# Linear term of the first batch by another route, and the weights' transposes moved into the main loop

## The chip, the cores and the metric

The kernel runs on one core of a Trainium2 chip. The metric is the device time of one execution in microseconds. Three runs of the kernel before took 329.71, 330.14 and 330.32 us; the median, 330.14 us, is what a prediction is measured against. A traced execution of its own spans 328.5 us, and the TensorE clock granted in it was full (1.00) from end to end.

Engines are named as the profile names them: PE is TensorE's matmul, PEld its weight load, DVE is VectorE, ACT is ScalarE, POOL is GpSimd, SP is SyncE.

## The reference

Four batches of N = 12544 rows of C = 128 columns go through an attention with m = 32 inducing rows, twice, and then through a two-branch maxout layer.

```python
scale = 1.0 / np.sqrt(C)
def mab(q, kv):
    s = scale * (q @ kv.transpose(0, 2, 1))
    s = s - s.max(-1, keepdims=True)
    a = np.exp(s)
    a /= a.sum(-1, keepdims=True) + 1e-09
    return a @ kv
h = mab(I, x)              # (B, 32, 128): the inducing rows attend to x
y = mab(x, h)              # (B, N, 128): x attends to h
h1, h2 = y @ w1, y @ w2    # w1, w2: 128 x 1024
out = np.maximum(h1, h2) @ w_out   # w_out: 1024 x 128
```

The kernel uses max(h1, h2) = h1 + relu(h2 - h1), and that y = a h with a of only 32 columns. With e the unnormalised second attention,

```
out = [ relu(e (h (w2 - w1))) w_out  +  e (h w1 w_out) ] / rowsum(e)
```

h (w2 - w1) is a 32 x 1024 matrix for each batch, called hwd. h w1 w_out is a 32 x 128 matrix for each batch, called m1: the linear term.

## The kernel before

Rows are taken in chunks of 128, and chunks in blocks of up to 16, split into four quarters of up to four chunks. Each quarter has its own 32 rows of the PE array.

The order of all instructions is worked out by the program as it is built, with a small clock model `ck` of PE, ACT, DVE and the eight PSUM banks. Its durations are constants in the code; they order the instructions and choose between ACT and DVE, and they synchronise nothing. The parts of a block:

- `stage(blk)`: scores of the block, four column-tiled matmuls, then exp on ACT into the tile `e2`;
- `phase(jobs)`: up to four jobs, one for each quarter, side by side on the array. A job "U" makes a PSUM bank of e2 · hwd, which ACT or DVE turns into relu (16 bit) in SBUF; a job "L" makes the linear term of a group;
- `final_one`: one matmul of a relu piece with w_out into the bank of its group (a quarter's chunks), eight for each chunk;
- `evict_group`: DVE multiplies by the reciprocal of the row sum, and SP stores.

A group's bank is first written by its "L" job, so its finals come after that. Only block 0's first group adds its linear term at the end. Where PE would wait for a bank, `keep_busy` fills with matmuls on a tile `warm`.

The weights of batch 0 (cuts are marked "..."):

```python
w2h = relup.tile([128, 4096], F16, name="w2h", tag="relu0")[:, 0:J]
w1h = relup.tile([128, 4096], F16, name="w1h", tag="relu1")[:, 0:J]   # pool relup: bufs=2 for each tag
...
def small_hwd(b, halves=(0, 1)):
    ...
    for half in halves:
        for n in range(2 if b == 0 and half == 0 else 1):
            w = 256 if b == 0 and half == 0 else 512
            ...
            if b == 0:
                nc.tensor.matmul(out=ps, lhsT=st[b]["hT4"], rhs=w2h[:, sl], start=True, stop=False)
                nc.tensor.matmul(out=ps, lhsT=st[b]["hT4"], rhs=w1h[:, sl], start=False, stop=True)
            ...
            if half == 0 and n == 0:
                ...   # DVE evicts
            else:
                ...   # ACT evicts
def small_m1(b):
    ...
    nc.tensor.matmul(out=ps[:, 0:128], lhsT=st[b]["hT4"], rhs=w1out, start=True, stop=True)
    ...               # DVE evicts to m1, and for batch 0 to m1bd as well
def weights_2():      # w1T: eight transposes of w1h, evicted half by DVE, half by ACT
    ...
def weights_3():      # w1out = w1 w_out: eight matmuls with w1T, evicted by ACT
    ...
```

w1h is negated in place on DVE before these run. The start of the main loop:

```python
nc.vector.tensor_scalar(out=w1h, in0=w1h, scalar1=-1.0, scalar2=None, op0=ALU.mult)
sums = small_h(0)
weights_2()
small_sums(*sums)
stage(blocks[0])
small_hwd(0, (0,))
blocks[0].staged = max(blocks[0].staged, st[0]["hwdr"])
small_hwd(0, (1,))
stage(blocks[1])
...
phase(plan_phase(False))
weights_3()
phase(plan_phase(False))
pending.append((small_m1, (0,)))
state["stage"] = 2
weights_1b()
while state["g"] < len(groups) or held:
    ...   # phases, finals, stages and the next batches' first attention, by ck
```

How a relu is given to an engine:

```python
if max(ck.act, ready) + 0.477 <= max(ck.dve, ready) + 0.597:
    nc.scalar.activation(out=dst, in_=src, func=AF.Relu)
    t = ck.on_act(ready, 0.477)
else:
    nc.vector.tensor_scalar(out=dst, in0=src, scalar1=0.0, scalar2=None, op0=ALU.max)
    t = ck.on_dve(ready, 0.597)
```

Of the kernel before, what the change touches and what calls it, by code (L numbers as in the profile page):

```python
# [9 lines left out]
F16 = mybir.dt.float16  # L10
F32 = mybir.dt.float32
AF = mybir.ActivationFunctionType
ALU = mybir.AluOpType
# [3 lines left out]
INF = 1e9  # L17
# [85 lines left out]
def kernel(  # L103
# [9 lines left out]
    nc = tc.nc  # L113
    B, N, C = x.shape
    M = inducing.shape[0]
# [26 lines left out]
    def bank(shape, dtype=F32, only=None):  # L142
        i = min(range(8), key=lambda j: ck.bank[j]) if only is None else only
        uid[0] += 1
        return i, psum.tile(shape, dtype, name=f"ps{uid[0]}", tag=f"bank{i}", bufs=1)
# [51 lines left out]
    with tc.manual_schedule(engines={ET.PE, ET.DVE, ET.Activation, ET.Pool, ET.SP}):  # L197
# [247 lines left out]
            nc.vector.tensor_scalar(out=st[0]["rw"], in0=st[0]["rs"], scalar1=1.0 / scale, scalar2=None, op0=ALU.mult)  # L445
            ck.bank[st[0]["eb"]] = st[0]["rsr"] = ck.on_dve(end, 0.34)

        def small_hwd(b, halves=(0, 1)):
            if 0 in halves:
                st[b]["hwd"] = smp.tile([128, J], F16, name=f"hwd_{b}", tag="hwd")  # L450
            hwd = st[b]["hwd"]
            for half in halves:
                for n in range(2 if b == 0 and half == 0 else 1):
                    w = 256 if b == 0 and half == 0 else 512
                    bi, ps = bank([128, 512])
                    ps = ps[:, 0:w]
                    sl = slice(512 * half + w * n, 512 * half + w * (n + 1))
                    ck.wait(max(ck.bank[bi], st[b]["hT4r"]), "p1")
                    if b == 0:
                        nc.tensor.matmul(out=ps, lhsT=st[b]["hT4"], rhs=w2h[:, sl], start=True, stop=False)  # L460
                        nc.tensor.matmul(out=ps, lhsT=st[b]["hT4"], rhs=w1h[:, sl], start=False, stop=True)
                        end = ck.run(0.43 * w / 512)
                    else:
                        nc.tensor.matmul(out=ps, lhsT=st[b]["hT4"], rhs=w21[:, sl], start=True, stop=True)  # L464
                        end = ck.run(0.215)
                    if half == 0 and n == 0:
                        if b == 0:
                            nc.vector.tensor_scalar(
                                out=hwd[:, sl], in0=ps, scalar1=st[0]["rw"], scalar2=None, op0=ALU.mult
                            )  # L470
                        else:
                            nc.vector.tensor_copy(out=hwd[:, sl], in_=ps)
                        ck.bank[bi] = ck.on_dve(end, 0.07 + w / 970.0)
                    else:
                        nc.scalar.activation(
                            out=hwd[:, sl], in_=ps, func=AF.Copy, scale=st[0]["rw"] if b == 0 else 1.0
                        )
                        ck.bank[bi] = ck.on_act(end, 0.06 + w / 1200.0)
                    st[b]["hwdr"] = max(ck.bank[bi], st[b].get("hwdr", 0.0))

        def small_m1(b):
            bi, ps = bank([128, 512])
            ck.wait(max(ck.bank[bi], st[b]["hT4r"]), "p1")
            nc.tensor.matmul(out=ps[:, 0:128], lhsT=st[b]["hT4"], rhs=w1out, start=True, stop=True)
            end = ck.run(0.06)
            m1 = smp.tile([128, C], F16, name=f"m1_{b}", tag="m1")
            bd = {0: [0], B - 1: [0, 1, 2, 3]}.get(b, [])
            outs = [(m1bd[32 * q : 32 * (q + 1), q, :], slice(32 * q, 32 * (q + 1))) for q in bd]
            for o, r in outs + [(m1, slice(0, 128))]:
                if b == 0:  # L490
                    nc.vector.tensor_scalar(
                        out=o, in0=ps[r, 0:128], scalar1=st[0]["rw"][r, :], scalar2=None, op0=ALU.mult
                    )
                else:
                    nc.vector.tensor_copy(out=o, in_=ps[r, 0:128])
                ck.bank[bi] = ck.on_dve(end, 0.2)
            st[b]["m1"] = m1
            st[b]["m1r"] = ck.bank[bi]
# [13 lines left out]
            for h in range(2):  # L512
                nc.gpsimd.tensor_sub(w21[:, 512 * h : 512 * (h + 1)], w_of[h][0], w_of[h][1])

        def weights_2():
            for g in range(2):
                bi, ps = bank([128, 4, 128], F16)
                ck.wait(ck.bank[bi], "w")
                for j in range(4):
                    jb = 4 * g + j  # L520
                    nc.tensor.transpose(ps[:, j, :], w1h[:, 128 * jb : 128 * (jb + 1)], identity16)
                end = ck.run(0.056 * 4)
                if g == 0:
                    nc.vector.tensor_copy(out=w1T[:, 0:4, :], in_=ps)
                    ck.bank[bi] = ck.on_dve(end, 0.4)
                else:
                    nc.scalar.copy(out=w1T[:, 4:8, :], in_=ps)
                    ck.bank[bi] = w_of["w1T"] = ck.on_act(end, 0.5)

        def weights_3():  # L530
            bi, ps = bank([128, 512])
            ck.wait(max(ck.bank[bi], w_of["w1T"]), "w")
            for jb in range(NJB):
                nc.tensor.matmul(
                    out=ps[:, 0:128],
                    lhsT=w1T[:, jb, :],
                    rhs=woutp[:, jb, :],
                    start=(jb == 0),
                    stop=(jb == NJB - 1),
                )  # L540
            end = ck.run(0.056 * NJB)
            nc.scalar.mul(out=w1out, in_=ps[:, 0:128], mul=-1.0)
            ck.bank[bi] = w_of["w1out"] = ck.on_act(end, 0.2)
# [24 lines left out]
        def stage(blk):  # L568
# [27 lines left out]
                scale=st[0]["rs"] if blk.b == 0 else scale,  # L596
            )
            blk.staged = ck.bank[bi] = ck.on_act(end, 0.05 + wd * 128 / 1200.0)
            blk.staged = max([blk.staged] + [st[qu.b].get("hwdr", 0.0) for qu in some])
        relu_of = {}  # L600

        def relu_slot(blk, q):
# [84 lines left out]
        weights_1()  # L687
        nc.vector.tensor_scalar(out=w1h, in0=w1h, scalar1=-1.0, scalar2=None, op0=ALU.mult)
        sums = small_h(0)
        weights_2()  # L690
        small_sums(*sums)
        stage(blocks[0])
        small_hwd(0, (0,))
        blocks[0].staged = max(blocks[0].staged, st[0]["hwdr"])
        small_hwd(0, (1,))
        stage(blocks[1])


        groups, ends = [], [0] * 4
# [199 lines left out]
        def phase(jobs):  # L899
# [6 lines left out]
            for (kind, q, a, u), bi in zip(jobs, free):  # L906
                _, ps = bank([128, 512], only=bi)
                ready = max(ck.bank[bi], a.blk.staged if kind == "L" else a.staged)
                if kind == "L":
                    ready = max(ready, st[a.blk.b]["m1r"])  # L910
                got.append((kind, q, a, u, bi, ps, ready))
# [47 lines left out]
            for kind, q, a, u, bi, ps, _ in got:  # L959
                ck.bank[bi] = INF  # L960
                if kind == "L":
                    a.bank, a.ps = bi, ps
                    state["lin"] += 1
                    continue
                _, t0, w, uu = u
                jpb = 4 // w
                w4 = a.quarters[q].w
                dst = a.relu[q][:, 0 : NJB * w4 * 128].rearrange("p (j t) -> p j t", j=NJB)
                dst = dst[:, uu * jpb : (uu + 1) * jpb, 128 * t0 : 128 * (t0 + w)]
                src = ps.rearrange("p (j t) -> p j t", j=jpb)  # L970
                ready = end + 0.03
                if max(ck.act, ready) + 0.477 <= max(ck.dve, ready) + 0.597:
                    nc.scalar.activation(out=dst, in_=src, func=AF.Relu)  # L973
                    t = ck.on_act(ready, 0.477)
                else:
                    nc.vector.tensor_scalar(out=dst, in0=src, scalar1=0.0, scalar2=None, op0=ALU.max)  # L976
                    t = ck.on_dve(ready, 0.597)
                ck.bank[bi] = t
                a.done[q, t0, uu] = t
                ptr[q][1] += 1  # L980
                state["issued"] += 1
# [4 lines left out]
        def at(n, f, *a):  # L986
            jobs_at.setdefault(n, []).append((f, a))
            if f in (pool_scores, pool_accum):
                due[f, a] = n
# [24 lines left out]
        def ready(f, a):  # L1014
# [16 lines left out]
                return d.get("esrr", INF) <= now  # L1031
            if f is small_h:
                return d.get("haccr", INF) <= now
            if f in (small_hwd, small_m1):
                if f is small_m1 and a[0] == 0 and w_of["w1out"] > now:
                    return False
                return d.get("hT4r", INF) <= now
            return True

        COL = (pool_scores, pool_accum)  # L1040
        FULL = (pool_rest, small_rep, small_h, small_hwd, small_m1)

        def side_work():
            while jobs_at and min(jobs_at) <= chunks_done[0]:
# [31 lines left out]
        def want_stage(ahead):  # L1076
# [10 lines left out]
                "hT4" in st[qu.b] and "hwd" in st[qu.b] for qu in blocks[k0].quarters if qu  # L1087
            )

        phase(plan_phase(False))  # L1090
        weights_3()
        phase(plan_phase(False))
        pending.append((small_m1, (0,)))
        state["stage"] = 2
        weights_1b()
        START = ck.pe
        while state["g"] < len(groups) or held:
# [63 lines left out]
```

The softmax here doesn't subtract the row's maximum and nothing guards it: scores larger than these inputs give would overflow.

## Time and profile before

| what | PE | ACT | DVE |
|---|---|---|---|
| busy of 328.5 us | 322.6 | 280.7 | 285.3 |
| finals, line L792, 3136 of them | 218.1 | | |
| phases, line L957: U jobs and L jobs | 89.0 + 38.8 | | |
| relus, lines L973 and L976 | | 244.6 (463) | 205.8 (321) |
| group evictions, line L819 (108) | | | 68.6 |

Matmuls overlap in the array, so their single lengths add up to more than the span. What counts for the PE is the distance from one to the next, which the chain of waits shows. In this kernel's lines L521 is a transpose in `weights_2`, L534 a matmul in `weights_3`, L440 the one in `small_sums`, L460 and L461 those of hwd for batch 0, L464 those of hwd for the other batches, L484 that of m1, L582 a `stage`, L957 a `phase`, L792 a final, L749 filler, L357 the column-tiled accumulation of a first attention, L248 the scores of batch 0's first attention. L475 is hwd's eviction on ACT, L594 the exp of `stage`.

The first 24 us load x, run the first attention of batch 0 and prepare the weights; the main loop follows to the end. Some 3 us after the last final the kernel is over.

### The profile page before, as it was taken

What the parts mean: (1) busy time and instruction counts of PE and PEld (TensorE: products, weight loads), DVE (VectorE), ACT (ScalarE), POOL (GpSimd) and SP (SyncE); (2) the same over time, 40 slices, a digit from 0 to 9 for tenths busy, and PEclk for the clock granted to TensorE, in tenths of its full rate; (3) what the DMA queues carried; (4) which work ended last, traced back from release to release, by engine and by line L of the source; (5) the groups of instructions that cost most, each with busy time, mean ns of one, the idle gap of its engine ahead of it and who ended that gap; (6) DMA issues with size and microseconds to landing.
All of it is one profiled execution on the core that took longest, in us unless ns stands there. A gap on an engine that the chain in (4) does not pass through costs nothing.

```text
span 328.5 us, 12601 instructions
## 1 busy us (share of the span) xinstructions
PE 322.6 (98%) x5401; PEld 244.1 (74%) x5401; DVE 285.3 (87%) x532; ACT 280.7 (85%) x562; POOL 25.7 (8%) x54
## 2 busy tenths in 40 slices
PE   8999999999999999999999999999999999999996
PEld 3876777777777777777777777777777777778785
DVE  3359899999988999998989989988989989989873
ACT  3679899998789999988888999998968999999961
POOL 7351030000310000000040000000000000000000
PEclk9999999999999999999999999999999999999999
DMA  8999999964299999672479999983212312222233
GB/s 207 208 206 213 289 237 205 216 187 124 57 227 244 229 221 213 167 155 97 132 139 245 226 257 215 197 177 100 98 66 97 114 67 99 98 98 98 80 116 114
DMA packets 70823, 53.65 MB, mean 163 GB/s; under 512 B 52176, under 2 KB 55408, under 8 KB 70768
## 3 DMA queue, kind: packets, MB, share of 16 engines
q1 hardware_dynamic: 64656, 38.63, 47.4%
q0 software_dynamic: 6112, 14.22, 22.1%
q8 instruction: 42, 0.69, 0.9%
q14 instruction: 13, 0.11, 0.1%
HBM read 28.33 MB, written 25.69 MB: 164 GB/s over the span
## 4 chain that ended last, share of the span: by engine, by line
PE 96%; DVE 1%; issue 1%; ACT 0%; DVEq 0%; ACTq 0%
PE ps L792 60%; PE ps L957 22%; PE ps L582 3%; PE ps L232 2%; PE ps L357 1%; PE ps L309 1%; PE ps L648 1%; PE ps L248 1%; PE ps L280 1%; PE ps L622 1%; DVE relu L976 1%; PE ps L749 1%; PE ps L271 1%; PE ps L640 0%; PE ps L464 0%
## 5 line engine op out<-in xcount | busy, mean ns | idle before, releaser
L973 ACT ACTIVATE relu<-ps 128x512 f16<-128x512 f32 x463 | 244.6, 604 | 31.1 <-PE ps L957 24.1
L976 DVE TENSOR_SCALAR relu<-ps 128x512 f16<-128x512 f32 x321 | 205.8, 681 | 18.8 <-PE ps L957 17.9
L792 PE MATMUL ps<-woutp,relu 128*128 128x128 f16 x3136 | 218.1, 220 | 0.0
L792 PEld LDWEIGHTS <-relu 128*128 128x128 f16 x3136 | 177.3, 98 | 39.4 <-issue 28.3
L957 PE MATMUL ps<-e,hwd 32*128 32x512 f16 (+2 forms) x880 | 89.0, 360 | 0.0
L819 DVE TENSOR_TENSOR o<-ps,rp 128x512 f32<-128x512 f32 (+3 forms) x108 | 68.6, 635 | 5.7 <-PE ps L792 3.1
L957 PEld LDWEIGHTS <-hwd 32*128 32x128 f16 x880 | 25.0, 91 | 21.1 <-issue 0.8
L957 PE MATMUL ps<-m,e 32*128 32x128 f16 x381 | 38.8, 217 | 0.0
L957 PEld LDWEIGHTS <-e 32*128 32x128 f16 x381 | 21.4, 92 | 2.6
L165 POOL DMA_DIRECT2D xn<-in_x_dram x31 | 16.7, 551 | 8.4 <-DMA xn<-in_x_dram 4.4
L236 DVE COPY xT<-ps 128x512 f16<-128x512 f16 (+3 forms) x11 | 5.5, 504 | 8.1 <-PE ps L232 8.0
L594 ACT ACTIVATE e<-ps 128x512 f16<-128x512 f32 (+2 forms) x21 | 11.6, 572 | 0.0
L320 ACT ACTIVATE eu<-ps 128x512 f16<-128x512 f32 x18 | 10.8, 619 | 0.0
L582 PE MATMUL ps<-xT,hT 128*32 128x512 f16 (+3 forms) x114 | 10.4, 366 | 0.0
L164 POOL COPY pace<-esr 128x1 f32<-128x1 f32 x2 | 0.4, 183 | 116.6 <-DVE esr L391 116.6
L239 ACT COPY xT<-ps 128x768 f16<-128x768 f16 (+3 forms) x11 | 6.1, 557 | 3.0 <-PE ps L232 2.9
L232 PE MATMUL ps<-identity,xn 128*128 128x128 f16 x98 | 7.7, 224 | 0.1
L582 PEld LDWEIGHTS <-hT 128*32 128x32 f16 x114 | 2.9, 93 | 5.9 <-issue 5.2
L232 PEld LDWEIGHTS <-xn 128*128 128x128 f16 x98 | 5.9, 100 | 1.3 <-DVE xn L644 0.9
L257 ACT ACTIVATE et<-ps 128x448 f16<-128x448 f32 (+4 forms) x11 | 4.5, 413 | 2.6 <-PE ps L248 2.6
L632 DVE RECIPROCAL rp<-ps 128x16 f32<-128x16 f32 (+2 forms) x28 | 6.7, 239 | 0.0
L622 PE MATMUL ps<-ones_q,e 128*128 128x4 f16 x102 | 6.5, 165 | 0.0
(96 smaller groups left out, 117.5 us busy)
## 6 DMA issues: line engine op xcount, KB each, us to landing
out_dram<-o SPq DMA_DIRECT2D x90, 256.0 KB, 2.5
xn<-in_x_dram POOLq DMA_DIRECT2D x24, 448.0 KB, 11.9
out_dram<-o SPq DMA_DIRECT2D x10, 128.0 KB, 3.1
xn<-in_moe_w_dram POOLq DMA_DIRECT2D x4, 256.0 KB, 14.1
xn<-in_x_dram POOLq DMA_DIRECT2D x4, 224.0 KB, 10.2
xT<-xn SPq DMA_TRANSPOSE x42, 3.8
xf<-in_x_dram SPq DMA_DIRECT2D x1, 512.0 KB, 3.7
xf<-in_x_dram SPq DMA_DIRECT2D x1, 384.0 KB, 4.1
```

Of the source, the lines that this page charges most:

```text
L165: nc.gpsimd.dma_start(out=xn_at[b, i][:, 0:n, :], in_=xr[b, :, k0 : k0 + n, :])
L232: nc.tensor.transpose(ps[:, j, :], xn[:, g + j, :], identity16)
L320: nc.scalar.activation(out=eu, in_=ps, func=AF.Exp, scale=scale, accum_out=st[b]["es"][:, u : u + 1])
L582: nc.tensor.matmul(out=ps[32 * q : 32 * (q + 1), 128 * t : 128 * (t + n)], lhsT=hq, rhs=xT[:, c : c + n, :], start=True, stop=True, tile_p ...
L594: nc.scalar.activation(out=blk.e2[:, 0 : 128 * wd], in_=ps[:, 0 : 128 * wd], func=AF.Exp, scale=st[0]["rs"] if blk.b == 0 else scale,)
L622: nc.tensor.matmul(out=ps[:, 4 * t : 4 * t + 4], lhsT=blk.e2[:, 128 * t : 128 * (t + 1)], rhs=ones_q, start=True, stop=True,)
L632: nc.vector.reciprocal(out=blk.rp[:, 0:wd, :].rearrange("p t q -> p (t q)"), in_=ps[:, 0 : 4 * wd])
L792: nc.tensor.matmul(out=g.ps[:, 128 * c : 128 * (c + 1)], lhsT=g.blk.relu[q][:, 128 * (jb * w4 + t) : 128 * (jb * w4 + t + 1)], rhs=woutp[: ...
L819: nc.vector.tensor_mul(osb[:, 0:n, :], g.ps[:, 0 : n * C].rearrange("p (s c) -> p s c", s=n), rp)
L957: nc.tensor.matmul(**seq[i])
L973: nc.scalar.activation(out=dst, in_=src, func=AF.Relu)
L976: nc.vector.tensor_scalar(out=dst, in0=src, scalar1=0.0, scalar2=None, op0=ALU.max)
```

## The change

It makes the linear term of batch 0 without w1 w_out: first (h w1), transposed, from eight small matmuls, then that times w_out, 32 column-tiled matmuls. So w1T and w1out aren't needed until batch 1, and their making goes behind chunk 16. hwd of batch 0 is made in four pieces of 256 columns, evicted by DVE and ACT in turn, and a phase waits only for the pieces that it reads. The second score tile goes behind the first phase. It is meant to let the main loop start sooner and to take work off its start.

```diff
-        def small_hwd(b, halves=(0, 1)):
+        def small_hwd(b, pieces=None):
+            w = 256 if b == 0 else 512
...
+            for n in range(J // w) if pieces is None else pieces:
...
+                for jb in range(w * n // 128, w * (n + 1) // 128):
+                    st[b]["hwdr", jb] = ck.bank[bi]
+        def small_hw1():
+            bi, ps = bank([128, 512])
+            ck.wait(max(ck.bank[bi], st[0]["hT4r"]), "p1")
+            for jb in range(NJB):
+                nc.tensor.matmul(
+                    out=ps[:, M * jb : M * (jb + 1)],
+                    lhsT=w1h[:, 128 * jb : 128 * (jb + 1)],
+                    rhs=st[0]["hT4"][:, 0:M], start=True, stop=True)
+            end = ck.run(0.056 * NJB)
+            hw1T = smp.tile([128, NJB, M], F16, name="hw1T", tag="hw1T", bufs=1)
+            nc.scalar.mul(out=hw1T.rearrange("p j m -> p (j m)"), in_=ps[:, 0 : NJB * M], mul=-1.0)
...
+        def small_m1_0(_=0):
...
+            for jb in range(NJB):
+                for q in range(4):
+                    nc.tensor.matmul(
+                        out=ps[32 * q : 32 * (q + 1), 0:128],
+                        lhsT=st[0]["hw1T"][:, jb, :], rhs=woutp[:, jb, :],
+                        start=(jb == 0), stop=(jb == NJB - 1),
+                        tile_position=(0, 32 * q), skip_group_check=True)
...   # DVE evicts to m1bd and m1, scaled by rw
-        def weights_2():
-            for g in range(2):
-                bi, ps = bank([128, 4, 128], F16)
...
+        def weights_2(_=0):
+            bi, ps = bank([128, NJB, 128], F16)
...   # eight transposes of w1h into one bank
+            nc.vector.tensor_copy(out=w1T, in_=ps)
...
-            blk.staged = max([blk.staged] + [st[qu.b].get("hwdr", 0.0) for qu in some])
...
         sums = small_h(0)
-        weights_2()
         small_sums(*sums)
         stage(blocks[0])
-        small_hwd(0, (0,))
-        blocks[0].staged = max(blocks[0].staged, st[0]["hwdr"])
-        small_hwd(0, (1,))
-        stage(blocks[1])
+        small_hwd(0, (0, 1))
...
+                if kind == "U":
+                    jpb = 4 // u[2]
+                    ready = max([ready] + [st[a.quarters[q].b]["hwdr", jb] for jb in range(u[3] * jpb, (u[3] + 1) * jpb)])
...
-                if max(ck.act, ready) + 0.477 <= max(ck.dve, ready) + 0.597:
+                if max(ck.act, ready) + 0.487 <= max(ck.dve, ready) + 0.608:
...   # the same two constants in the lines below it
+        small_hwd(0, (2, 3))
         phase(plan_phase(False))
-        weights_3()
+        stage(blocks[1])
+        state["stage"] = 2
+        small_hw1()
         phase(plan_phase(False))
-        pending.append((small_m1, (0,)))
-        state["stage"] = 2
+        pending.append((small_m1_0, (0,)))
+        at(16, weights_2, 0)
+        at(18, weights_3, 0)
         weights_1b()
```

`at(n, f)` makes a piece of side work due once n chunks are evicted; `weights_2`, `weights_3` and `small_m1_0` run when the clock model has them ready, PE is in its full mode and a bank is free.

## The prediction

> **What bounds the kernel now.** I read the page first, then the waits of the long middle, the chain of waits from 21 to 60 us, and the timelines of ACT and DVE around the start of the main loop. The page says that three engines are nearly full:
>
> ```profile
> PE 322.6 (98%) x5401; PEld 244.1 (74%) x5401; DVE 285.3 (87%) x532; ACT 280.7 (85%) x562; POOL 25.7 (8%) x54
> ```
>
> Shares don't say which of them ends the kernel. The waits between 60 and 290 us do:
>
> ```profile
> PEld L792 <- issue: 22.0, 94, 0.4
> ACT relu L973 <- PE ps L957: 18.2, 40, 1.1
> DVE relu L976 <- PE ps L957: 12.6, 35, 0.9
> ```
>
> ACT and DVE wait for the PE (18.2 and 12.6 us); the PE waits for neither, its only large entry is "issue", its own turn from one kind of matmul to the next. So in the middle the PE's queue is the clock: every matmul put there costs its own length, every one taken away gives it back. At the start of the main loop it is otherwise; the chain of waits, in order of time (start, length, what):
>
> ```profile
> 21.77 0.09 PE ps L280 x3
> 21.86 0.45 PE ps L521 x8
> 22.32 0.17 PE ps L440 x2
> 22.49 0.58 PE ps L582 x4
> 23.07 0.22 PE ps L460
> ...
> 24.05 0.33 PE ps L582 x4
> 24.38 0.33 PE ps L957 x5
> 24.70 0.56 PE ps L534 x8
> 25.26 0.64 PE ps L957 x6
> ...
> 26.54 0.22 PE ps L749 x2
> ...
> 27.68 0.72 PE ps L749 x5
> 28.40 0.33 PE ps L957 x4
> 28.72 0.65 PE ps L749 x5
> 29.38 0.37 PE ps L957 x6
> ```
>
> L749 is filler[...]: 13 of them, 0.22 + 0.11 + 0.72 + 0.65 = 1.70 us, and none after 29.4 us. Up to 29.4 us the PE waits for relu evictions and for the first linear terms; from then on the chain is PE work without a hole. The time is therefore the moment at which the PE becomes gapless (29.4 us), plus the PE work that is left. The eviction engines in that stretch:
>
> ```profile
> 24.09 0.69 ACT L475 ACTIVATE hwd<-ps,rw 128x512 f16<-128x512 f32 x1
> 24.67 0.68 ACT L594 ACTIVATE e<-ps,rs 128x512 f16<-128x512 f32 x1
> 25.24 1.08 ACT L973 ACTIVATE relu<-ps 128x512 f16<-128x512 f32 x2
> ```
>
> On DVE relus run from 24.81 us without a stop (four to 27.32 us); on ACT the second half of hwd and the second score tile stand ahead of its relus.
>
> **What the Trainium skill says.** "Perfetto Trace Analysis", section "Identifying the Most-Contended Engine", warns that matmul busy share is no measure, and to look at weight loads: 74% here, so 98% PE isn't the array at its peak. I use the waits for that reason. The same page, "Optimization Strategy", says the engine that binds can change with the regime; the trace agrees (evictions before 29.4 us, PE after). "TensorE: Matmul & The Clock Gate", "Back-to-back issue gap", gives about 56 ns for an isolated warm 128-column matmul and 81 ns for a stream that has a weight load each. The trace sides with the smaller: eight transposes take 0.45 us in the chain, 56 ns each. "TensorEngine Tiling (Array Packing)", "PSUM Bottleneck", says that tiling speeds the PE and not the eviction; the first ten microseconds of the loop show it, with fillers while both eviction engines run.
>
> **The change part by part.**
>
> 1. w1's transposes (weights_2) leave the path before the first phase. They cost 0.45 us there, but behind them the row-sum matmul (L440, begins 22.16) needs a copy that ACT makes from 21.81 to 21.97 us. Without the transposes L440 can begin near 22.03, so the path gains only 22.16 - 22.03 = 0.13 us. The two evictions of w1T (DVE 0.42, ACT 0.59 us) lay in idle time.
>
> 2. The second score tile goes behind the first phase: 0.33 us of PE off the path (24.05 to 24.38). The first phase then waits for hwd's second piece on ACT, which ended at about 24.09; 0.11 to 0.13 earlier that is 23.97, plus some 0.08 to be seen, 24.05. The old first phase began loading at 24.31. Gain 0.26 us for parts 1 and 2 together.
>
> 3. hwd in four pieces: the columns stay 2048 (eight matmuls of 256 in place of four of 256 and two of 512). The fourth piece on ACT takes a pitch of 0.38 us (23.71 to 24.09 for a piece of 256) in place of 0.58 (24.09 to 24.67); DVE takes the third in idle time.
>
> 4. What the evictions make of it. DVE: relus from about 24.55 in place of 24.81, four done at 27.1 in place of 27.3. ACT: free at 23.97 + 0.38 = 24.35, waits for the first phase until 24.55, two relus at a pitch of 0.54 (the pair at 25.24 takes 1.08), then the score tile 0.57, the new copy of h w1 about 0.25 (estimate, between w1out's pitch of 0.16 and a 256-column piece's 0.38), two relus: 24.55 + 1.08 + 0.57 + 0.25 + 1.08 = 27.5. Before, its first four were done at 27.47. So DVE gains 0.2 us, ACT nothing; half a stage of the quarter microsecond survives. I put the gapless point 0.2 us earlier.
>
> 5. The linear term of batch 0. Gone: one matmul of 0.06 us and a wait for w1out. New: eight matmuls of 32 columns (the row L248 does seven in 0.24 or less, so about 0.25) and 32 column-tiled ones of 128 columns (the chain shows L357 x32 at 0.56), with one or two extra turns of about 0.1 us (eight matmuls of 56 ns make 0.45, and w3 took 0.56: the 0.11 between is the turn). w3's 0.56 us leaves the same stretch. Sum: 0.25 + 0.56 + 0.15 - 0.56 - 0.06 = +0.34 us, against 1.7 us of filler that it can displace. Mostly hidden. But m1 isn't ready earlier: w1out was copied by 26.5 us, the copy of h w1 ends near 26.4 by the sum in 4 (25.63 + 0.57 + 0.25), and 0.5 us of matmuls follow in place of 0.06. The second group's finals cannot begin before its linear phase (29.31 us before). I charge +0.1.
>
> 6. Moved into the gapless part: eight transposes 0.45 and eight matmuls 0.45 (w3's 0.56 less its turn), all on the PE: +0.9 us. One DVE copy of 128x1024 fp16 (0.69 us, as the largest xT copy L236) and the w1out copy (0.30 on ACT) land on engines that wait for the PE there, so they're free.
>
> 7. w1h now lives until chunk 16 or later, and it is one of only two buffers with the tag relu1. Until then the second quarter's relu tiles can share only the other. Block 1's first write would wait for block 0's second group (its 24th final falls at about 31.1 us, the relu would begin about 31.0): nearly nothing. Block 2's (phase at 40.70) would wait for block 1's second group, near 42.4: one relu held about a microsecond on one engine, part of which reaches the PE through the PSUM banks. +0.1 on average.
>
> 8. The eviction constants rise together (0.477 to 0.487 and 0.597 to 0.608). The real pitches are 0.54 and 0.64, so the new ones are nearer. Their ratio hardly moves; the order of phases and finals is redrawn a little through the whole kernel. A phase more or less is two turns, about 0.2 us. Somebody who nudges such constants has probably looked for a good order for this start: -0.3, with at least 0.5 either way.
>
> Sum: -0.2 + 0.1 + 0.9 + 0.1 - 0.3 = +0.6 us. 330.14 + 0.6 = 330.7 us.
>
> **The rivals.** (a) The early start is worth more than I grant: relus start earlier on both engines, and if the first linear phase comes one phase sooner, most of the last 0.65 us of filler goes, and more behind it. For it: the second group's finals wait on m1 alone. Against: the copy of h w1 stands on ACT behind two relus and a score tile, and the 32 matmuls come on top. Then -0.2 becomes -1.2, and the time 329.6 to 329.8. (b) The shared buffer of part 7 is the main cost: the held relu keeps a PSUM bank, the next phase lacks a fourth bank, the PE stops. For it: 1 us is an estimate from the old order; if block 2's relu comes earlier against the finals, it is 2 or 3. Against: the PE's relus are several phases ahead there. Then 331.5 to 333. (c) The redrawn order decides and the start matters little: 330.1 plus or minus 0.7. (d) The moved weights work is hidden after all, because near chunk 16 the PE would otherwise wait: 329.8. Against: between 36 and 44 us the chain has no filler and no wait.
>
> **Range and chances.** Parts 1 to 6 have little spread, some 0.4 us; parts 7 and 8 and rival (a) bring it to about 1 us. Eight in ten: 329.3 to 332.0. A change of 2% is 6.6 us. Nothing here can give that, since all that the change shortens lies in 2.5 us of path and 1.7 us of filler; losing that much would take a repeated stall on the buffer. Faster by over 2%: 0.01; within: 0.975; slower: 0.015.
>
> **What would show it.** The first phase (L957's successor) loading near 24.05; ACT relus from 24.6; fillers of 1.2 to 1.8 us in all, ending near 29.2; transposes of w1h and the product with w_out standing among finals near 43 us, 0.45 us each, with no filler beside them; a relu of the second quarter near 41 us that waits for a final. I am wrong if the fillers fall below 0.7 us (the linear term came sooner), if the gapless point lies before 28.8 us, or if the PE shows a wait for PSUM of over 0.5 us after 32 us.

## The result and the profile after

The changed kernel takes 334.3 us (median of 6 runs, 333.45 to 334.99) against 330.23 us before (6 runs, 329.71 to 330.8). The ratio is 1.012, with an interval from 1.0099 to 1.0141. It is 4 us slower, and lies outside the range that I gave.

The page of the kernel after, its row of engines (busy time, share of the span, instructions):

```profile
PE 325.9 (98%) x5448; PEld 245.6 (74%) x5448; DVE 289.1 (87%) x540; ACT 277.7 (83%) x555; POOL 25.7 (8%) x54
```

The PE has 3.3 us more busy time, and it is still the engine without room. ACT lost seven relus, 463 to 456, and DVE gained them. The waits between 60 and 290 us (engine, line, what it waited for; total us, times, longest):

```profile
ACT relu L1001 <- PE ps L985: 23.6, 62, 1.1
PEld L817 <- issue: 22.1, 94, 0.4
DVE relu L1004 <- PE ps L985: 12.2, 30, 0.9
...
PEld L817 <- DVE relu L1004: 1.5, 5, 0.4
...
PEld L817 <- ACT relu L1001: 0.3, 1, 0.3
```

In these lines L817 is a final, L985 a phase, L1001 and L1004 are the relus on ACT and DVE. The last two lines are new: six finals wait for a relu (1.8 us), and ACT waits 5.4 us longer for the PE than before. So the eviction engines have more slack, and the PE still arrives too early at some finals. I took this for a matter of order and not of a missing engine; e3 below puts it to the test.

The chain of waits at the start of the main loop (start, length, what). L774 is filler, L505 the 32 column-tiled matmuls of the new linear term, L555 and L564 w1's transposes and their product with w_out:

```profile
22.62 0.38 PE ps L440 x2
23.01 0.33 PE ps L612 x4
...
24.32 0.36 PE ps L985 x4
...
24.70 1.96 DVE relu L1004 x3
...
26.93 0.56 PE ps L505 x32
...
28.10 0.33 PE ps L774 x3
...
29.98 0.70 PE ps L774 x5
30.68 0.37 PE ps L985 x4
31.05 0.37 PE ps L817 x4
31.42 0.04 DVEq L1004
...
31.50 0.70 DVE relu L1004
...
43.22 0.45 PE ps L555 x8
...
46.25 0.45 PE ps L564 x8
```

Three things are to be seen. The first phase stands directly behind one score tile and hwd, as meant. The fillers did not become fewer: 13 of the kernel's 19 stand here, as before, and the last begins at 31.6 us, where the last one before began at 29.1; 0.6 us of that is this execution's later start (21.87 against 21.27 us at the point described below). Six more stand near 178 and 252 us, where the kernel before had none. And at 31.42 the chain leaves the PE: a phase waits for a bank that a DVE relu holds. The timeline of DVE says why that relu came late (in brackets the idle time before it, and what ended it):

```profile
30.19 0.69 DVE L1004 TENSOR_SCALAR relu<-ps 128x512 f16<-128x512 f32 x1
31.50 1.29 DVE L1004 TENSOR_SCALAR relu<-ps 128x512 f16<-128x512 f32 x2 [0.62 <-PE ps L817]
```

The only thing that a relu shares with an earlier *final* in this program is its output buffer, which the final reads; so this relu waited for its buffer. That is the pair of buffers from which w1h now takes one, and e1 below tests it.

To compare executions I measure from a point before anything that was changed, the start of the last exp (L257) of batch 0's first attention. Worked out from the traces so, in us:

| kernel | first phase | first L job | 25th final | 113th | 209th | last |
|---|---|---|---|---|---|---|
| before | 3.04 | 8.05 | 9.83 | 18.55 | 27.42 | 303.70 |
| after | 2.38 | 6.49 | 9.37 | 18.52 | 28.64 | 306.69 |

The early start is real: 0.66 us at the first phase, 1.56 at the first linear job. About a quarter of a microsecond of both is this one profile of the kernel before, which is late: five kernels below that have its start have 2.79 and 7.78 to 7.81. The lead is gone by the 113th final, 1.2 us are lost by the 209th, and 1.8 more in the long rest. A further 0.6 us lies behind the last final (0.3 in the second profile of the changed kernel).

### The profile page after: what moved, and what is told of

Its sections match the earlier page's. It is cut to its first block, busy times and chain, and to the rows that moved or that the text cites. A ratio compares the mean times of both kernels' runs of the same rounds, so it can differ in the third digit from the quotient of the medians.

```text
span 332.7 us, 12706 instructions
## 1 busy us (share of the span) xinstructions
PE 325.9 (98%) x5448; PEld 245.6 (74%) x5448; DVE 289.1 (87%) x540; ACT 277.7 (83%) x555; POOL 25.7 (8%) x54
## 4 chain that ended last, share of the span: by engine, by line
PE 95%; DVE 3%; ACT 1%; issue 0%; DVEq 0%; ACTq 0%
PE ps L817 59%; PE ps L985 22%; PE ps L612 2%; PE ps L232 2%; DVE relu L1004 2%; PE ps L309 1%; PE ps L357 1%; PE ps L677 1%; PE ps L248 1%; PE ps L280 1%; PE ps L651 1%; PE ps L669 1%; PE ps L271 1%; PE ps L774 0%; DVE m1bd L531 0%
## 5 line engine op out<-in xcount | busy, mean ns | idle before, releaser
L1001 ACT ACTIVATE relu<-ps 128x512 f16<-128x512 f32 x456 | 241.9, 602 | 34.9 <-PE ps L985 27.8
L1004 DVE TENSOR_SCALAR relu<-ps 128x512 f16<-128x512 f32 x328 | 210.9, 680 | 19.0 <-PE ps L985 15.6
L817 PE MATMUL ps<-woutp,relu 128*128 128x128 f16 x3136 | 218.6, 220 | 0.4 <-DVE relu L1004 0.2
L817 PEld LDWEIGHTS <-relu 128*128 128x128 f16 x3136 | 177.4, 98 | 40.7 <-issue 28.8
L985 PE MATMUL ps<-e,hwd 32*128 32x512 f16 (+2 forms) x880 | 89.8, 360 | 0.1
L985 PEld LDWEIGHTS <-hwd 32*128 32x128 f16 x880 | 24.9, 91 | 21.7 <-issue 1.9
L985 PE MATMUL ps<-m,e 32*128 32x128 f16 x381 | 38.8, 217 | 0.0
L985 PEld LDWEIGHTS <-e 32*128 32x128 f16 x381 | 21.4, 92 | 2.8
L257 ACT ACTIVATE et<-ps 128x448 f16<-128x448 f32 (+4 forms) x11 | 4.5, 413 | 2.6 <-PE ps L248 2.6
L309 PE MATMUL ps<-xT,inducingT 128*32 128x512 f16 x72 | 6.5, 385 | 0.1
```

The costliest lines, as they stand in the source:

```text
L309: nc.tensor.matmul(out=ps[32 * g : 32 * (g + 1), :], lhsT=inducingT, rhs=xT_tiles[b % 2][:, U * u + 4 * g : U * u + 4 * (g + 1), :], start ...
L817: nc.tensor.matmul(out=g.ps[:, 128 * c : 128 * (c + 1)], lhsT=g.blk.relu[q][:, 128 * (jb * w4 + t) : 128 * (jb * w4 + t + 1)], rhs=woutp[: ...
L985: nc.tensor.matmul(**seq[i])
```

## The experiments

Each was timed beside the kernel before, whose median was 330.32 to 330.38 us in every group. "New constants" are 0.487 (ACT) and 0.608 (DVE), "old" ones 0.477 and 0.597.

**The four first questions.** e0_after_again is the changed kernel, not edited, run beside the others of this group.

> The changed kernel once more, unedited, as the base for the three beside it. Expected 334.3 us, between 333.4 and 335.0, 1.2% over the kernel before. Its second profile tells which of the +0.6 us before the first phase and the +0.6 us behind the last final in the first profile belongs to the kernel: theory 'single execution' expects the last exp of the first attention back near 21.3 us (it began at 21.87 against 21.27 before), theory 'kernel' expects 21.9 again.

334.21 us (333.74 to 334.64), 1.011 [1.0094, 1.0127]. The loss repeats. In the second profile the last exp begins at 21.78 us, near the 21.87 of the first. Even so this is no cost of the change: in the nine profiles with the same instructions up to there (the kernel before and eight of the experiments) it begins anywhere from 20.99 to 21.97. From that exp on, the two profiles of the changed kernel agree closely (last final at 306.69 and 306.73), so this measure tells apart differences that the spread of whole executions hides.

e1_own_w1 takes the long life away from the shared buffer: the negated w1 is written to a tile that is free by then.

```diff
-nc.vector.tensor_scalar(out=w1h, in0=w1h, scalar1=-1.0, scalar2=None, op0=ALU.mult)
+w1n = xn_tiles[2].rearrange("p k c -> p (k c)")[:, 0:J]
+nc.vector.tensor_scalar(out=w1n, in0=w1h, scalar1=-1.0, scalar2=None, op0=ALU.mult)
+w1h = w1n
```

> The negated w1 is written to a tile of the first attention that is free by then, in place of back into one of the two buffers of the second quarter's relus; the order of all instructions is the same. Theory 'buffer': the wait of a DVE relu for a final at 30.9 to 31.5 us (0.62 us) and the phase behind it that lacks a bank (0.78 us in the chain), and part of the stretched phase at 43.7, go: 0.8 to 1.3 us faster than the changed kernel, 333.1 to 333.5. Theory 'order': the buffer's wait is made up by filler or lead, and the time moves by less than 0.3 us.

334.11 us (332.94 to 334.45), 1.0101 [1.0078, 1.0124]. Against e0 nothing that can be told from the spread; two of the four executions ran at a mean granted clock of 0.995 (334.4 us, see the last section) and the other two took 332.94 and 333.78, while none of e0's ran at the lower clock. Its chain at the same place (L776 filler, L819 finals, L987 phases):

```profile
30.63 0.33 PE ps L776 x3
30.96 0.33 PE ps L987 x4
...
31.29 0.73 PE ps L819 x10
32.02 0.34 PE ps L987 x4
```

The stop at 31.4 us is gone, finals run on into the next phase, and by the 209th final e1 is 0.71 us ahead of e0. In this profile the gain is then lost again: at 71 us an exp on ACT waits for a transfer, `eT<-eu`, for 0.9 us that the kernel after hasn't got. That wait need not belong to the order, for e2 below keeps the order and hasn't got it. So the buffer costs 0.7 us at its place; how much of it is left at the end with these constants isn't shown, but it is not the main part of 4 us.

e2_own_w1_no_w1out is e1 without the eight transposes, the product and both evictions behind chunk 16; the time that the clock model books for them stays, so the order stays. w1out is zero: the linear terms of batches 1 to 3 are left out of the result.

```diff
-                nc.tensor.transpose(ps[:, jb, :], w1h[:, 128 * jb : 128 * (jb + 1)], identity16)
+                pass
 ...   # the product and the two evictions likewise
+        nc.gpsimd.memset(w1out, 0.0)
```

> As the one before, and the eight transposes of w1, the product with w_out and their two evictions are left out at their place behind chunk 16, the order of all else the same; w1out is zero, so the linear terms of batches 1 to 3 are missing. Theory 'PE is the clock': 0.9 us faster than the kernel with the free buffer (16 matmuls at 56 ns). Theory 'hidden': under 0.3 us.

333.95 us (332.52 to 334.02), 1.0092 [1.0069, 1.0116]. The 0.2 us less than e1 is not like against like, since three of the four executions ran at 0.995: those took 0.5 us less than e1's at that clock, and the one at full clock, 332.52, took 0.4 and 1.3 less than e1's two. The profiles say where. Up to the 400th final, behind the place of the work, e2 is 0.17 us ahead of e1, of 0.9 us of matmuls; 0.8 more comes at 71 us, where its exp doesn't wait for a transfer. So the moved work costs little, and isn't the main cause either.

e3_before_new_constants is the kernel *before* with the two new constants and nothing else.

```diff
-if max(ck.act, ready) + 0.477 <= max(ck.dve, ready) + 0.597:
+if max(ck.act, ready) + 0.487 <= max(ck.dve, ready) + 0.608:
 ...   # and in on_act, on_dve
```

> The kernel before with the two eviction constants of the change alone (0.487 and 0.608). Theory 'order': the redrawn order by itself costs 1 to 2 us, as the changed kernel lost 1.77 us behind its 208th final: 331.2 to 332.2. Theory 'start': the constants are neutral, 329.7 to 330.7, and the loss behind the 208th final comes from what the change does at the start and the new side work.

333.68 us (333.56 to 334.45), 1.0101 [1.0082, 1.0120]. Two numbers that no instruction carries cost 3.35 us by themselves. Its waits between 60 and 290 us (L792 finals, L957 phases):

```profile
ACT relu L973 <- PE ps L957: 24.0, 60, 1.1
PEld L792 <- issue: 20.9, 90, 0.4
DVE relu L976 <- PE ps L957: 12.4, 29, 0.9
...
PEld L792 <- DVE relu L976: 2.0, 6, 0.5
...
PEld L792 <- ACT relu L973: 1.1, 3, 0.4
```

It is the picture of the kernel after, in a kernel that has nothing else of the change: ACT waits 24 us for the PE, nine finals wait for relus. And filler is back in the middle, here two microseconds after the eviction of the next batch's hwd, which DVE begins at 93.50 us (L749, chain of waits):

```profile
95.44 0.22 PE ps L749 x2
95.66 0.33 PE ps L957 x4
```

**Which part of the constants, and what they cost in place.** e4_after_old_constants is the changed kernel with the old constants, e5_own_w1_old_constants is e4 with e1's edit.

> The changed kernel with the eviction constants of before (0.477 and 0.597), all else of the change kept. Theory 'constants': the two constants cost 3.4 us on the kernel before and most of that here; 330.6 to 331.8, the rest being 0.9 us of moved weights work and some 0.8 us of the shared buffer, less the earlier start. Rival 'parts': the constants were tuned to the new start, so without them the changed kernel is no faster, 333.5 to 335.

> As the one before, with the negated w1 in a tile of its own. Theory 'buffer': 0.3 to 0.9 us faster than with the shared buffer, 329.9 to 331.2; with the earlier start it may equal the kernel before. Rival 'absorbed': whatever the start gains is lost at a later wait that comes at its own time (a DMA), and the two are equal within 0.3 us.

e4: 331.94 us (331.01 to 332.87, 17 runs), 1.0043 [1.0031, 1.0055]. e5: 331.37 us (330.86 to 332.25, 8 runs), 1.003 [1.0015, 1.0046]. In place the constants cost 334.2 - 331.9 = 2.3 of the 4 us, and with the old order the shared buffer costs 331.94 - 331.37 = 0.57 us (331.38 - 331.05 = 0.33 without the executions at a mean clock of 0.994 or 0.995). The second is hardly clear of the scatter.

The profiles show where each part is lost. In us from the start of the last exp (e8 and e11 come below):

| kernel | constants | 1000th final | last final, the 3136th | between |
|---|---|---|---|---|
| before | old | 104.22 | 303.70 | 199.48 |
| e8 | old | 103.76 | 303.27 | 199.51 |
| e4 | old | 105.11 | 304.64 | 199.53 |
| e11 | old | 104.76 | 304.28 | 199.52 |
| after | new | 105.13 | 306.69 | 201.56 |
| e3 | new | 104.59 | 306.90 | 202.31 |

With the old constants the long rest takes 199.5 us whatever else of the change is there; from the 800th final on, each final of e4 comes 0.89 to 0.95 us behind the same one of the kernel before. With the new constants the rest takes 2.1 and 2.8 us more (good to about a microsecond, since finals change places in another order). So most of what the constants cost is lost in the rest, and all else that the change costs is lost by the 800th final.

e6_before_act_constant raises only ACT's constant in the kernel before (0.487, 0.597), e7_before_dve_constant only DVE's (0.477, 0.608). My theory after e3 was that relus moved from ACT to the slower DVE.

> The kernel before with ACT's constant alone raised (0.487 and 0.597). The program then gives ACT 449 relus in place of 463 and has 28 filler matmuls in place of 13. Theory 'split': each relu moved from ACT (0.54 us) to DVE (0.64 us) loads the engine that also evicts the groups, and DVE's backlog is what stops the PE: 14 moved relus cost more than the 10 of both constants, 334 to 336. Rival 'chance of order': no relation to the split, anything between 330 and 334.

> The kernel before with DVE's constant alone raised (0.477 and 0.608): 469 relus on ACT in place of 463, 13 fillers as before, but four more visits to the column mode (42 for 38). Theory 'split': no DVE backlog, the only cost is the visits at about 0.3 us each, 330.5 to 331.7. Rival 'chance of order': anything between 330 and 334.

e6: 333.15 us (333.1 to 334.32), 1.0088 [1.0065, 1.0112], with 449 relus on ACT. e7: 332.42 us (332.26 to 332.61), 1.0058 [1.0042, 1.0075], with 469 on ACT, six more than the kernel before. More relus on the faster engine, and 2 us slower: the theory of the share fell.

e9_before_halfway_constants sets both halfway, 0.482 and 0.602, in the kernel before.

> The kernel before with both constants half way (0.482 and 0.602): 490 turns, 39 column visits, 15 fillers, 465 relus on ACT, all near the counts of before (489, 38, 13, 463). Theory 'counts': the loss follows the turns and column visits of the order that results, so 330.3 to 331.3. Rival 'chance': the counts say nothing, and any other order than the tuned one costs 2 to 3.5 us.

331.95 us (331.47 to 332.21), 1.0049 [1.0036, 1.0062], with 465 relus on ACT. A step of one per cent in two constants costs 1.6 us. Its profile is of the fastest of the four executions and shows only 0.5 us of it up to the last final; where the others lose the rest isn't known.

e10_new_constants_no_late_filler is e3 without its eight fillers behind chunk 40; the clock model still books their time. The rival was that the PE would not have waited there.

```diff
-            for _ in range(n):
+            for _ in range(n if chunks_done[0] < 40 else 0):
```

> The kernel before with the new constants, and the eight filler matmuls that its order has behind chunk 40 left out, nothing else moved. They take 1.16 us on the PE. Theory 'filler costs': PE isn't waiting there, so 1 us faster than with them, near 332.6. Rival 'filler fills': PE would wait for a relu there in any case, 333.5 to 334.0.

333.55 us (333.42 to 334.42), 1.0105 [1.009, 1.0119]: 0.13 us less than e3, where the eight fillers alone take about 1.16. The filler stands where the PE waits in any case, so it is a sign of the loss and not its cause.

**The other half of the change alone.** e8_pieces_and_score_tile is the kernel before, old constants, with only hwd in four pieces, a phase that waits for its own pieces, and the second score tile behind the first phase. w1out and its linear term are those of before.

```diff
 sums = small_h(0)
 weights_2()
 small_sums(*sums)
 stage(blocks[0])
-small_hwd(0, (0,))
-blocks[0].staged = max(blocks[0].staged, st[0]["hwdr"])
-small_hwd(0, (1,))
-stage(blocks[1])
+small_hwd(0, (0, 1))
 ...
+small_hwd(0, (2, 3))
 phase(plan_phase(False))
+stage(blocks[1])
+state["stage"] = 2
 weights_3()
```

> One half of the change alone, on the constants of before: hwd in four pieces with readiness by piece, and the second score tile behind the first phase; w1's transposes, w1out and the linear term stay as before. The program keeps 489 turns between the PE's modes, 38 visits to the column mode and 13 fillers, as before. Theory 'order': with the order kept, the start is a quarter of a microsecond shorter and nothing is added: 329.7 to 330.3, equal to the kernel before or up to 0.5 us faster. Rival: relus in the first 5 us bind, nothing is gained, 330.2 to 330.6.

330.28 us (329.82 to 331.06, 14 runs), 0.9999 [0.9991, 1.0008]. Its order counts as many turns, fillers and relus per engine as the one before. By the measure of the table above its first phase came at 2.46 us, its 113th final at 18.09, its last at 303.27, 0.43 us ahead of the kernel before. A quarter of a microsecond of that is the late profile of before: in the five kernels that keep its start and have other constants (e3, e6, e7, e9, e10) the 113th final comes at 18.29 to 18.31, so 0.2 us are gained, and kept. In the median nothing of it can be seen: executions of one kernel differ by more than that.

**What is left, at the old constants.** e14_old_constants_no_w1out is e5 with e2's omission (again no linear term in batches 1 to 3). e11_clock_guard is e5 with two matmuls of 512 columns on the warm tile put where the transposes stood before:

```diff
 sums = small_h(0)
+_, ps = bank([128, 512])
+for _ in range(2):
+    nc.tensor.matmul(out=ps, lhsT=warm[:, 0:128], rhs=warm, start=True, stop=True)
 small_sums(*sums)
```

> The changed kernel with the old constants and w1 in a tile of its own, and two matmuls of 512 columns on the warm tile where the transposes of w1 stood, without moving anything else. In three of eight executions of that kernel the granted clock averaged 0.994 to 0.995, one stretch of 3.4 us at half speed from the start of the main loop, and those took 332.1 to 332.3 in place of 330.9 to 331.6; the kernel before had none in 24. Theory 'idle PE': the PE has too little to do before the first phase once the transposes are gone; with the two matmuls no execution shows the half-speed stretch, median 331.0. Rival 'chance of the die': a third still show it, median 331.4.

> The changed kernel with the old constants and w1 in a tile of its own, with w1's transposes, the product with w_out and their evictions left out behind chunk 16 and the order of all else kept; w1out is zero, so the linear terms of batches 1 to 3 are missing. Theory 'moved work': 0.9 us less than with them, 330.0 to 330.5, as the kernel before. Rival 'start': the loss lies in the linear term's own 40 matmuls and turns, 330.9 to 331.4.

e11: 331.14 us (330.59 to 331.83, 7 runs), 1.0026 [1.0014, 1.0039]; what it guards against is told in the last section. e14: 331.35 us (330.4 to 331.95, 20 runs), 1.0027 [1.0019, 1.0036], the same as e5. The two chains show where the 0.9 us of w1's work went. e11, with the work (L555, L564; L990 are phases):

```profile
42.23 0.45 PE ps L555 x8
...
42.84 0.33 PE ps L990 x4
...
44.56 0.45 PE ps L564 x8
...
45.40 0.33 PE ps L990 x4
```

e14, without it (L980 phases):

```profile
42.96 0.74 PE ps L980 x4
...
45.48 0.67 PE ps L980 x4
```

A phase of four row-tiled matmuls takes 0.33 us. Where the work is left out the two phases take 0.74 and 0.67: the PE comes to them sooner and then waits in them. The timeline of ACT in e14 shows 14 relus in one stretch of 7.20 us there, so ACT is full as well, and the stretch that I took for PE alone has room for side work. From the start of the last exp to the last final it is 303.96 us in e14 and 304.28 in e11: 0.3 of 0.9 us paid, half of that by the 209th final.

**Turns as a guide.** Old and new constants differ in how often the PE turns between its full, row-tiled and column-tiled modes (489 turns, of them 38 visits to column mode, in the kernel before; 492 and 42 in e3). To test it I took e8 with ACT's constant at 0.479 (e12_fewer_turns, 488 and 37) and at 0.475 (e13_more_turns, 495 and 44); DVE's stays 0.597.

> The neutral half of the change (four pieces, second score tile behind the first phase) with ACT's constant at 0.479: 488 turns and 37 column visits in place of 489 and 38, no filler behind the 208th final. Theory 'counts': one column visit less is worth 0.3 us, 329.9 to 330.2, the fastest of all. Rival 'waits': the order has waits that the counts don't show, 330.5 to 332.

> The same with ACT's constant at 0.475: 495 turns and 44 column visits, no filler behind the 208th final either. Theory 'counts': with the mean turn lengths of the traces (0.225 us from a phase to the finals, 0.15 back, 0.27 into and out of the column mode) 1.9 us more than 489 turns, 331.9 to 332.4. Rival 'waits': the loss isn't tied to the counts, anything from 330.3 to 334.

e12: 329.5 us (329.29 to 330.09, 9 runs), 0.9975 [0.9965, 0.9985]. It beats both kernels. e13: 332.86 us (331.93 to 333.87), 1.0073 [1.0046, 1.0101]. The waits of e12 between 60 and 290 us (L789 finals):

```profile
PEld L789 <- issue: 22.6, 97, 0.4
...
ACT relu L973 <- PE ps L957: 16.5, 35, 1.1
DVE relu L976 <- PE ps L957: 11.9, 32, 1.0
```

ACT waits 7 us less than in the kernel after, and no final waits for a relu. The direction came out right twice, but not by the count: e9 has 490 turns and 39 visits, one more of each than the kernel before, and loses 1.6 us; and of the 3.7 us by which e13's profile is behind e8's at the last final, 3.0 are one stop near 69 us, told below. So the count is not shown to be the cause in either.

## Why the prediction was wrong

I predicted +0.6 us and the change costs 4. A chain of runs divides the 4 us by medians: constants 2.3 (e4 against e0), shared buffer 0.57 (e5 against e4), half clock in some executions 0.23 (e11 against e5), the linear term from h w1 with w1's moved work 0.86 (e11 against e8), and nothing for pieces and score tile (e8). Each difference is good to a few tenths. Their sum is no check, because it is e0 less e8 by construction. The last finals of the profiles give 2.1 for the constants, 0.4 for buffer and guard together, and 1.0 for the linear term with the moved work. The 2.3 and the 0.86 are clear of the scatter; the 0.57 and the 0.23 are not, and only one of the ten executions of the changed kernel as it stands had the half clock.

**The step that failed is part 8.** I wrote "The real pitches are 0.54 and 0.64, so the new ones are nearer" and "Somebody who nudges such constants has probably looked for a good order for this start: -0.3". Measured it is +2.3 us in place and +3.35 on the kernel before, where nothing else was changed. The sign was taken from a guess about intentions and the size from "a phase more or less is two turns". Of six other settings tried on the kernel before, or on its twin e8, five cost 1.6 to 3.4 us and one gained 0.8: the old values sat near a narrow good spot, and being nearer to the real pitches bought nothing. The opening reading, that the time is the moment of the gapless PE plus the PE work left, has no place for such a cost: e3 has the work of the kernel before. What the new order costs, worked out from the distances between successive matmuls in e3 and before, behind the 209th final: waits that filler stands in for 1.3 us, waits inside phases 0.9, turns into and out of column mode about 1.8, and -0.3 in the rest, of 3.8 us. Rival (c), that the order decides, was the right one, with the wrong range (330.1 ± 0.7). Why one order makes more relus late than another is only counted here, not explained; two theories of it, the share of relus per engine and the number of turns, fell or held only roughly.

**Parts 1 to 4** hold in the trace. The first phase came 0.58 us earlier in e8 against the kernel before by the table's measure. Some of that is the profiled execution of before, which lost about 0.25 us there: e3, with the same start, has 2.79. That leaves 0.33 against my 0.26. ACT does its score tile and the copy of h w1 in the order that I had, behind two relus that begin at 24.81 us. The "0.2 us earlier" is 18.29 (e3) to 18.09 (e8) at the 113th final. It is too small for the medians.

**Part 5** sized the work rightly (32 matmuls 0.56 us at 26.93), and "m1 isn't ready earlier" holds: DVE finishes writing m1 at 6.35 us by the table's measure, against 6.38 in e3 with the old start. What came sooner is its use: the first L job runs 0.14 us behind it in place of 1.4. So rival (a) had the event right and its worth wrong. At the old constants the linear half of the change costs 0.86 us, where parts 5 and 6 made +1.0 of it.

**Part 6** charged +0.9. The work stands where I put it, 0.45 us each at 43.22 and 46.25, without filler beside it. But e14 shows that the PE was not gapless there, and only about 0.3 us is paid in the profiles and none in the medians: rival (d) was mostly right on this term. So it was luck that parts 5 and 6 together came out near their sum: something else in this half costs about half a microsecond, and as the finals of e11 and e8 show it does so before the 800th final (from there on e11 is 0.99 to 1.03 us behind e8). It is open whether that is again the order, which the pieces of work redraw (492 turns and 40 visits).

**Part 7** called block 1's wait "nearly nothing" and feared block 2. It was the other way round: the stop was at block 1 (31.42 us), 0.8 us of PE. At the old constants that is 0.57 us in the median (0.33 at equal clock), for which I had charged 0.1; at the new ones 0.7 at the 209th final, and 0.1 in the medians, which mix two clocks. Rival (b) had the mechanism, a bank held by a late relu, and too large a size.

None of my three signs of being wrong was met as written. The fillers of the start stayed far above 0.7 us (13 in number, as before), the gapless point came later and not earlier, and the stop for a bank, 0.82 us, began at 31.42 us, ahead of the mark of 32 that I had set, so that only a quarter of a microsecond of it lies behind the mark. None of them looked at the long middle, where 1.8 of the 3.0 us between the two profiles lie. A list of signs that covers only the edited region can't catch a part whose reach is the whole kernel.

## What to carry to other kernels

When instructions are ordered at build time by a cost model, treat a change of its constants as a change of the whole program and time it by itself, first: here a step of about two per cent in two constants was worth more than all the reordered work. Size such a term by its spread over a few nearby values, not by its intention. And before giving a long-lived tile a slot of a rotating pair, find the first user that then has to wait for the *other* slot.

## What was not expected of the hardware

Some executions ran a stretch at half of the granted TensorE clock. The windows of e5's profile show one (window; its length; busy time of PE, PEld, DVE, ACT, POOL; granted clock; DMA share; GB/s):

```profile
22.00:23.00 1.00, 0.90 (x9) 0.63 (x10) 0.59 (x3) 0.18 (x2) 0.11 (x1) 1.00 1.17 208
23.00:24.00 1.00, 1.00 (x8) 0.67 (x5) 0.48 (x1) 0.98 (x2) 0.42 (x1) 0.52 1.15 223
...
25.00:26.00 1.00, 1.00 (x20) 0.55 (x17) 1.00 (x2) 0.96 (x2) 0.00 (x0) 0.50 1.08 215
...
27.00:28.00 1.00, 0.81 (x38) 0.62 (x39) 0.92 (x3) 0.96 (x2) 0.00 (x0) 1.00 1.10 215
```

The front of a kernel is a case of its own: in the profile of before, for which I gave the clock as full from end to end, the matmuls of 512 columns on the warm tile take 607 to 634 ns up to 4.6 us and 379 from 5.9 us on, though the record has no granted clock for the first of these. The stretch of e5 stands in the middle of work. It lasts 3.41 us, from 23.07 to 26.48 by the start times of the matmuls, just where the transposes are gone, with nine matmuls in the microsecond ahead of it (27 between 20 and 21 us); e5's first phase comes 0.58 us later than e11's by the table's measure. e5's executions with a mean granted clock of 0.994 or 0.995 have a median of 332.1 us, those at 0.999 or above 331.05. In the kernels with this start 20 of 63 executions had such a mean, 15 of the 36 with w1 in a tile of its own. Of the kernel before, of e8 and of e12, where eight transposes fill the place, none did, and none of e11's seven with two matmuls in it; at 15 in 36, seven without one would come by chance about once in forty times. The place is known only where a profile caught it. The Trainium skill ("TensorE: Matmul & The Clock Gate", Part 1, "What's actually happening") gives half rate after an idle window of about 3.4 us. The length of the slow stretch agrees. The condition doesn't: in e5 the PE is busy for 12.5 of the 13.1 us ahead of it.

e13's profile has the other case (waits between 66 and 74 us, then windows, columns as above, and one line of PE's timeline with the idle time before it):

```profile
ACT eu L320 <- DMA eT<-eu: 2.5, 1, 2.5
```

```profile
69.00:71.00 2.00, 0.55 (x7) 0.15 (x4) 1.31 (x3) 0.59 (x2) 0.00 (x0) 1.00 0.63 149
71.00:73.00 2.00, 1.85 (x20) 1.65 (x19) 0.03 (x1) 2.00 (x6) 0.00 (x0) 0.55 0.61 178
73.00:75.00 2.00, 2.00 (x21) 1.26 (x21) 1.75 (x3) 1.33 (x4) 0.00 (x0) 0.59 0.54 154
```

```profile
71.15 0.56 PE L957 MATMUL ps<-e,hwd 32*128 32x512 f16 x1 [1.60 <-ACT eu L320]
```

An exp waits 2.5 us for a transfer, ACT's queue stops behind it, the PE idles for 1.6 us, and then runs 3.4 us at half clock. Between the 320th and the 560th final this profile falls 3.0 us behind e8's, so a stop of 1.6 us costs nearly twice its length. The transfer is not late: by the measure of the tables it lands at 48.77 us, and at 48.44 in e8. There the exp begins only at 49.16; in e13 the order has ACT free for it at 46.35. In that kernel two executions at 0.994 to 0.995 take 333.8 us and two others 331.9.
